# A fused sliding-window attention and long-convolution kernel: spectral sums in pairs, three third spectra by adding copies, quartered output tails, regrouped weights of v

## The chip, the core and the metric

The kernel runs on one core of a Trainium2 chip. A core has five engines that work side by side, each through its own queue in order: TensorE (PE in the profile, with its weight loads as PEld), VectorE (DVE), ScalarE (ACT), GpSimd (POOL) and SyncE (SP), which here only issues transfers. Matmul results land in PSUM; everything else lives in the on-chip memory or in HBM. The metric is the device time of one execution in microseconds.

## What is computed

Two independent parts, concatenated on the last axis. B = 1, S = 2048, D = 576.

```python
# A: 32 heads of 18; query s sees keys s, s-2, ..., s-14
qkv = x @ wqkv                                  # 2048 x 576 times 576 x 1728
logits = einsum("bhsd,bhswd->bhsw", q, kg) * scale     # w = 8 gathered keys
attn = softmax(where(mask, logits, -1e9))
a = einsum("bhsw,bhswd->bhsd", attn, vg) -> (s, 576) @ wo

# B: H3-like long convolution, per channel
k_shift = sum over t of k[s - t] * shift_k[:, t]       # 4 taps
kv = k_shift * v
y = irfft(rfft(kv, 4096) * rfft(ssm_k, 4096))[:2048] + kv * ssm_D
b = q * y
out = concatenate([a, b], axis=-1)
```

## The kernel before

**Part B in blocks.** Time is cut into four blocks of 512. DVE makes kv of a block (`taps`, L558 to L562), PE and ACT fold it (`mirror`, L570 and L571) and make its spectrum with cosine and sine tables (`x_spectrum`, L692; ACT writes it at L695, names fx0 to fx3). The four filter blocks are folded (`fold_filter`, L615 to L620) and transformed (`filter_spectrum`, L589 and L590, ACT at L635); a spectrum is turned from one block to the next by an accumulating copy on POOL's queue (`turn_filter`, L649). A spectrum has two parts of HB = 2304 elements per partition, and a third, their sum. Products of two spectra are then three elementwise products (parts one, two and three) in place of four, as in the three-multiplication form of a complex product. Where a block first needs its third part, DVE adds it (L1122): in three pieces of 768 for block 0, in one add of 2304 for the x spectra 1, 2, 3 and the filter spectra 1, 2, 3.

**The spectral stage.** Output block j needs the products of x block i with filter block j - i for all i up to j, in three thirds t of the channels: 30 products, in the order j, t, i. `products` (L985) is one DVE instruction of 3 x 768 elements into one of three buffers `pr`. `sums` (L1006) adds the three parts with 16 matmuls of 64x64 tiles, four at a time in the array's quarters, into two accumulators in PSUM; on the last i of a third, ACT copies both out (L1019; DVE the very last, L1017). `inverse` (L1038, last block's end L1057) and its back turn (L1079, L1065) make the time signal, and DVE multiplies it with q (L1092, at the end L1047). q is loaded by POOL's queue (L974, L976) and the result stored by SP's.

**Part A.** Projections of q, k and v (`project`, bodies at L360 and L364, 64-row tails at L371 and L377; `dest` gives the place). q and k use 128-column weight tiles. For v (comp 2) the weights are read in steps of nine, 64 columns at a time, straight from the loaded matrix (`wa`), so that channels of one residue mod 9 lie together and a v tile holds the rows in the order that the attention needs; two such 64-column tiles run side by side. Logits are DVE products of q and shifted k (L745) summed by PE (L754), softmax runs on DVE and ACT (L773 to L789), the attention weights are spread to all rows by SP's copies (L824), DVE multiplies with v (L846), PE sums (`weigh`, L862 and L876), and `output` multiplies with wo: L915 for 128 rows, `tails` at L907 for the 64 rows that are left, as two matmuls of 64 rows by 128 columns. ACT copies out (L922) into one of two buffers `st` behind wo in `qk`, and ACT's queue stores (L926).

**What sets the order.** Everything on one engine runs in the order in which the program issues it. DVE's list is the backbone. PE work that may be moved (projections, spectra, inverses, outputs) stands in a deque `units`; at each call of `until()` the next number of the table `PLACES` says how many of them are issued there. `FKS` and `FXS` mix filter spectra, x spectra and v's projections in that deque. `need(label)` issues units until none of that label is left. In the spectral stage the products run LEAD = 2 ahead of the sums, and `sums` calls `until()` once per product:

```python
for n, (j, t, i) in enumerate(todo):
    produce(n + LEAD)
    if (t, i) == (0, 0):
        need(f"inv{j - 2}")
    r = sums(j, t, i, *prs.pop(n))
```

Of the kernel before, what the change touches and what calls it, by code (L numbers as in the profile page):

```python
# [16 lines left out]
PSUM = bass.MemoryType.PSUM  # L17

PLACES = (
    16, 8, 5, 17, 0, 2, 0, 5, 2, 2, 1, 2, 8, 1, 0, 10, 0, 2, 3, 4, 2, 1, 2, 1, 2, 1, 0, 4, 3, 2, 12, 0, 4, 5, 2,  # L20
    2, 2, 2, 7, 1, 0, 2, 2, 0, 1, 0, 1, 0, 0, 1, 0, 2, 2, 1, 6, 1, 0, 2, 0, 2, 0, 1, 2, 0, 4, 1, 0, 1, 0,
)

FKS = (
    4, 0, 0, 3, 2, 0, 0, 0, 0, 0, 0, 0, 0, 0, 0, 0, 0, 0, 0, 0, 0, 0, 0, 0, 0, 0, 0, 0, 0, 0, 0, 0, 0, 0,
)
FXS = (
    6, 4, 3, 0, 0, 0, 0, 3, 2,
)


# [6 lines left out]
def kernel(  # L38
# [13 lines left out]
    nc = tc.nc  # L52
# [75 lines left out]
    def wa(kb, a):  # L128

        return view(xw, w_at(kb, 2) + a, [[9, 64]])  # L130

    def load_w(eng, comp, to=None):
        low, high = (to[:, 0:4, :], to[:, 4, :]) if to is not None else \
# [221 lines left out]
    def project(comp, jj):  # L355
        def body(ps, ct, jj, jp, first):
            for kb in range(4):
                se = dict(start=(kb == 0 and not first), stop=(kb == 3 and first))
                if ct < 4 and comp < 2:
                    nc.tensor.matmul(ps[:, jp, :], wq(kb, comp, 128 * ct, 128), xT(kb, 1024 * jj + 512 * jp, 512), **se)  # L360
                    continue
                for e in range(2):
                    w = wa(kb, min(2 * ct + e, 8)) if comp == 2 else wq(kb, comp, 512, 64)
                    nc.tensor.matmul(ps[64 * e:64 * e + 64, jp, :], w, xT(kb, 1024 * (jj if ct < 4 else e) + 512 * jp, 512),  # L364
                                     tile_position=(0, 64 * e), **se)

        def tails(ps, ct, jj, first):
            se = dict(start=first, stop=not first)
            if ct < 4 and comp < 2:
                for r in range(2):  # L370
                    nc.tensor.matmul(ps[:, r, :], wq(4, comp, 128 * ct, 128)[64 * r:64 * r + 64],  # L371
                                     x5(jj)[64 * r:64 * r + 64], tile_position=(64 * r, 0), **se)
                return
            for e in range(2):
                w = wa(4, min(2 * ct + e, 8)) if comp == 2 else wq(4, comp, 512, 64)
                for r in range(2):
                    nc.tensor.matmul(ps[64 * e:64 * e + 64, r, :], w[64 * r:64 * r + 64],  # L377
                                     x5(jj if ct < 4 else e)[64 * r:64 * r + 64], tile_position=(64 * r, 64 * e), **se)

        def unit(ct, jj, jp, first, box):  # L380
            t, o, pad = dest(comp, ct)
            if jp == 0:
                box["ps"] = bank2("ps_proj", "A")
                if first:
                    tails(box["ps"], ct, jj, True)
            ps = box["ps"]
            body(ps, ct, jj, jp, first)
            if jp == 0:
                clk["P"] += 1.15 if first else 0.9
                return  # L390
            if not first:
                tails(ps, ct, jj, False)
            pe(0.9 if first else 1.15, "A", 1.02)
            nc.scalar.activation(view(t, o + pad + 1024 * jj, [[512, 2], [1, 512]]), ps[:], ACT.Copy)  # L394
            if ct == 4 and comp > 0:
                nc.scalar.dma_start(view(t, o, [[1, PAD]])[64:128, :], view(t, o + 1024, [[1, PAD]])[0:64, :])

        for ct in range(4) if jj < 2 else [4]:
            first = ct % 2 == 1 if ct < 4 else comp == 1
# [251 lines left out]
    def turn_filter(m):  # L651
        for part in range(2):
            add_half(Ks, k_at(m, part), k_at(m - 1, part))

    for i in range(NBL):
        r = taps(i)
        until()
        if i < 2:
            load_k(i + 2)
            load_v(i + 2)  # L660
        if i == 1:
            load_filter(0)
            load_w(nc.sync, 2)
            for m in range(1, NBL):
                load_filter(m)
        if i == 1:
            nc.scalar.preload_act_table_set("natural_log_exp_and_others")
# [217 lines left out]
    spread(1)  # L885
    spread(2)

    wo = view(qk, 13312, [[2 * D, 2], [D, 2], [1, D]])
    woh = view(qk, 13312 + 4 * D, [[1, D]])
# [9 lines left out]
    def output(j, sb, h):  # L899

        hh, o = sb // 2, 128 * (sb % 2)
        ps = bank2("ps_wo", "A")

        def tails(first):
            for r in range(2):
                x = 64 * ((r + j) % 2)
                nc.tensor.matmul(ps[:, r, 0:HD], oTh(hh, r)[x:x + 64, o:o + 128],  # L907
                                 woh[x:x + 64, HD * h:HD * h + HD], start=first, stop=not first,
                                 tile_position=(x, 0))

# [69 lines left out]

    def products(j, t, i):

        pr = view(*((av, 0), (v, 6912), (qk, 9216))[npr[0] % 3], [[QTR, 3], [1, QTR]])
        npr[0] += 1
        r = dve(3 * QTR, lambda: nc.vector.tensor_tensor(  # L985
            pr, view(xw, HB * XG[i] + QTR * t, [[HB, 3], [1, QTR]]),
            view(Ks, k_at(j - i, 0) + QTR * t, [[HB, 3], [1, QTR]]), ALU.mult))
        return pr, r

    acc = {}  # L990

    def sums(j, t, i, pr, ready):

        until()
        m = j - i
        for r in range(2):
            sign = ((1, 1), (-1, 1), (-1, -1), (1, -1))[m][r]
# [111 lines left out]
    LEAD = 2  # L1109
    prs = {}  # L1110

    def produce(n):
        if n < len(todo):
            j, t, last = todo[n]
            for i in range(last + 1):
                need(f"fx{i}")
            due(1.0)
            for new, tile_, at in ((last == 0, Ks, k_at(j, 0)), (last == j, xw, HB * XG[j])):
                if new and (j == 0 or t == 0):
                    at, w = (at + QTR * t, QTR) if j == 0 else (at, HB)  # L1120
                    a, b, c = (view(tile_, at + HB * part, [[1, w]]) for part in range(3))
                    dve(w, lambda: nc.vector.tensor_tensor(c, a, b, ALU.add))  # L1122
# [5 lines left out]
    for n in range(LEAD):  # L1128
        produce(n)
    for n, (j, t, i) in enumerate(todo):  # L1130
        produce(n + LEAD)
        if (t, i) == (0, 0):
# [45 lines left out]
```

## Time and profile before

| | |
|---|---|
| median of 3 runs | 221.6 us (221.13 to 221.75) |
| the profiled execution | 221.13 us, its span 219.4 us |
| PE busy | 206.3 us, 94% of the span |
| DVE busy | 200.3 us, 91% |
| ACT busy | 151.6 us, 69% |
| POOL busy | 48.9 us, 22% |
| TensorE clock | 1.0 of full speed over the span |
| moved by DMA | 32.59 MB, mean 149 GB/s |

The span is what the profiler sees of the program on the core; 1.7 us lie around it. Busy times add up the durations of an engine's instructions. A matmul's duration holds its way through the array, so a busy PE may still have been waiting; how far one start is from the next is the better measure. "Idle before" a group is the engine's idle time ahead of its instructions, with what ended it.

The stages, read from the timelines: tables, taps, projections of q and k to about 57 us; logits and softmax of both halves with filter and x spectra and v's projections between them to about 124 us; weighing and outputs to about 157 us; the spectral stage to about 212 us; the last gate and stores.

### The profile page before, as it was taken

The page shows a single profiled execution, that of the slowest core. Times are in us where ns is not written, and L with a number is a line of the kernel's source. Part 1 is how long each engine was busy: PE and PEld are TensorE (multiplying, and loading weights), DVE is VectorE, ACT ScalarE, POOL GpSimd, SP SyncE. Part 2 cuts the span into 40 slices and gives each one's busy share as a digit, 9 for nine tenths or more (in the row PEclk, how much of TensorE's full clock was granted, in tenths as well). Part 3 has the DMA queues.
Part 4 walks back from the last instruction along what each step waited for, and adds up shares of the span by engine and source line. Part 5 has one row for each costly group of instructions (what it writes and reads, how often), then busy time and mean ns, then how long its engine had stood idle before and what let it go on. Part 6 is the DMA issues. An engine that isn't in the chain of part 4 may idle for free.

```text
span 219.4 us, 5341 instructions
## 1 busy us (share of the span) xinstructions
PE 206.3 (94%) x2262; PEld 119.1 (54%) x2266; DVE 200.3 (91%) x159; ACT 151.6 (69%) x218; POOL 48.9 (22%) x93
## 2 busy tenths in 40 slices
PE   7999899999699999999999999999979999999891
PEld 3543344444455556565576777555546666666560
DVE  7969999999989949899898699999999999999982
ACT  3699766896686799965359888755487776756530
POOL 8989800000320206220640000000240001130000
PEclk9999999999999999999999999999999999999999
DMA  6999987999150035999999485481282103580034
GB/s 211 269 282 276 266 286 253 158 200 253 28 87 4 0 54 82 189 178 221 226 249 236 59 232 133 68 183 55 74 249 74 40 4 108 172 251 13 3 100 115
DMA packets 32295, 32.59 MB, mean 149 GB/s; under 512 B 17136, under 2 KB 28016, under 8 KB 32272
## 3 DMA queue, kind: packets, MB, share of 16 engines
q1 hardware_dynamic: 25902, 21.93, 41.2%
q0 software_dynamic: 3744, 7.82, 17.8%
q10 hardware_dynamic: 2626, 2.52, 3.4%
q8 instruction: 17, 0.28, 0.5%
q14 instruction: 6, 0.05, 0.1%
HBM read 13.11 MB, written 4.72 MB: 81 GB/s over the span
## 4 chain that ended last, share of the span: by engine, by line
PE 72%; ACT 15%; DVE 7%; issue 3%; DVEq 0%; ACTq 0%
PE ps_proj L364 10%; PE ps_proj L360 7%; PE ps_acc L862 7%; PE ps_wo L915 6%; PE ps_z L1006 6%; PE ps_inv L1038 5%; PE ps_fx L692 4%; PE ps_log L754 4%; PE ps_fk L589 3%; PE ps_proj L482 3%; ACT Ks L635 2%; ACT xw L695 2%; PE ps_rev L615 2%; ACT qk L394 2%; PE ps_proj L377 2%
## 5 line engine op out<-in xcount | busy, mean ns | idle before, releaser
L745 DVE TENSOR_TENSOR av<-qk 128x4096 bf16<-128x4096 bf16 (+1 forms) x20 | 40.5, 2074 | 4.3 <-PE ps_log L754 4.2
L360 PE MATMUL ps_proj<-xw 128*128 128x512 bf16 x93 | 22.6, 380 | 0.8 <-ACT qk L394 0.5
L364 PE MATMUL ps_proj<-xw 128*64 128x512 bf16 x176 | 23.0, 396 | 0.0
L1019 ACT ACTIVATE av<-ps_z 128x768 bf16<-128x768 f32 x23 | 17.4, 809 | 5.3 <-PE ps_z L1006 5.3
L695 ACT ACTIVATE xw<-ps_fx 128x576 bf16<-128x576 f32 x32 | 18.5, 665 | 2.0 <-PE ps_fx L692 2.0
L974 POOL DMA_DIRECT2D TB<-in_B_q_dram x4 | 3.0, 742 | 75.7 <-DVE qk L846 45.4
L635 ACT ACTIVATE Ks<-ps_fk 128x576 bf16<-128x576 f32 x32 | 18.3, 660 | 1.7 <-PE ps_fk L590 1.5
L394 ACT ACTIVATE qk<-ps_proj 128x1024 bf16<-128x1024 f32 x14 | 14.4, 1027 | 7.0 <-PE ps_proj L371 3.7
L364 PEld LDWEIGHTS <-xw 128*64 128x64 bf16 x176 | 14.7, 180 | 7.3 <-issue 5.2
L915 PE MATMUL ps_wo<-qk 128*128 128x288 bf16 x128 | 18.1, 287 | 0.4 <-ACT qk L866 0.4
L692 PE MATMUL ps_fx<-xw,TB 64*128 64x288 bf16 x256 | 17.8, 283 | 0.2 <-ACT xw L571 0.2
L589 PE MATMUL ps_fk<-Ks,TB 128*128 128x384 bf16 x64 | 17.2, 327 | 0.1
L394 ACT ACTIVATE v<-ps_proj 128x1024 bf16<-128x1024 f32 x9 | 9.2, 1025 | 11.4 <-PE ps_proj L377 7.0
L561 DVE TENSOR_TENSOR xw<-xw,tB 128x2304 bf16<-128x2304 bf16 x12 | 16.3, 1358 | 0.4
L1038 PE MATMUL ps_inv<-av,TI 128*128 128x288 bf16 (+1 forms) x112 | 16.1, 292 | 0.6 <-ACT av L1019 0.6
L558 DVE TENSOR_TENSOR tB<-kj,skb 128x2304 bf16<-128x2304 bf16 x12 | 16.3, 1356 | 0.3
L620 POOL DMA_DIRECT2D Ks<-Ks x4 | 5.0, 1242 | 50.8 <-ACT Ks L618 50.8
L590 PE MATMUL ps_fk<-Ks,TB 128*128 128x192 bf16 x64 | 15.7, 246 | 0.0
L692 PEld LDWEIGHTS <-TB 64*128 64x128 bf16 x256 | 12.1, 94 | 6.5 <-issue 4.3
L922 ACT ACTIVATE qk<-ps_wo 128x576 bf16<-128x576 f32 x16 | 10.4, 650 | 7.3 <-PE ps_wo L907 4.5
L862 PE MATMUL ps_acc<-av,ident 64*64 64x512 bf16 x160 | 15.3, 378 | 0.1
L1041 ACT ACTIVATE v<-ps_inv 128x576 bf16<-128x576 f32 (+1 forms) x14 | 9.5, 675 | 8.3 <-PE ps_inv L1038 8.3
(187 smaller groups left out, 455.2 us busy)
## 6 DMA issues: line engine op xcount, KB each, us to landing
kj<-in_B_k_dram SPq DMA_DIRECT2D x7, 504.0 KB, 5.4
Ks<-Ks POOLq DMA_DIRECT2D x6, 576.0 KB, 8.3
TB<-av SPq DMA_DIRECT2D x12, 256.0 KB, 5.2
vt<-in_B_v_dram SPq DMA_DIRECT2D x8, 288.0 KB, 4.3
out_dram<-qk ACTq DMA_DIRECT2D x8, 288.0 KB, 2.4
Ks<-av SPq DMA_DIRECT2D x8, 256.0 KB, 5.1
xw<-in_A_wqkv_dram SPq DMA_DIRECT2D x3, 576.0 KB, 5.6
Ks<-in_A_x_dram SPq DMA_DIRECT2D x2, 576.0 KB, 5.2
```

Source lines behind the costliest of these rows:

```text
L360: nc.tensor.matmul(ps[:, jp, :], wq(kb, comp, 128 * ct, 128), xT(kb, 1024 * jj + 512 * jp, 512), **se)
L364: nc.tensor.matmul(ps[64 * e:64 * e + 64, jp, :], w, xT(kb, 1024 * (jj if ct < 4 else e) + 512 * jp, 512), tile_position=(0, 64 * e), **se)
L394: nc.scalar.activation(view(t, o + pad + 1024 * jj, [[512, 2], [1, 512]]), ps[:], ACT.Copy)
L589: nc.tensor.matmul(o[:, 0:2], w, rhs[:, 0:2], start=start, stop=stop)
L635: nc.scalar.activation(view(Ks, k_at(m, cs ^ (m & 1)) + 96 * gi, [[768, 3], [384, 2], [1, 96]]), acc3(ps), ACT.Copy, scale=(PSG, MSG)[cs][ ...
L692: nc.tensor.matmul(ps[:, pm, 0:HD], TX[64 * pm:64 * pm + 64, c, 128 * gi:128 * gi + 128], kv[64 * pm:64 * pm + 64, c, HD * h:HD * h + HD], ...
L695: nc.scalar.activation(view(xw, HB * XG[i] + 96 * gi + 1152 * h, [[HB, 2], [384, 3], [1, 96]]), view(ps, 0, [[512, 2], [96, 3], [1, 96]]), ...
L745: r = dve(1024 * nj, lambda: nc.vector.tensor_tensor(view(prod, 0, [[256 * nj, 4], [256, nj], [1, 256]]), view(t, o + 256 * hh, [[0, 4], [ ...
L862: nc.tensor.matmul(acc[64 * o:64 * o + 64, h, :], ident[64 * h:64 * h + 64, 64 * h:64 * h + 64], view(P, 256 * u, [[2048, 2], [1, 256]])[6 ...
L915: nc.tensor.matmul(ps[:, r, 0:HD], oT(hh, j + 2 * r, t)[:, o:o + 128], wo[:, t // 2, t % 2, HD * h:HD * h + HD], start=(t == 0 and h == 0) ...
L1019: nc.scalar.activation(y, z, ACT.Copy)
L1038: nc.tensor.matmul(ps[:, c, 0:n], TI[:, sl, pm, 128 * c:128 * c + 128], Yall[:, j % 2, pm, sl, c0:c0 + n], start=(pm == 0 and sl == 0), st ...
```

## The change

It has five parts.

- **Sums in groups of two.** Neighbouring products of one third are grouped (i even with the i behind it; the very last product stands alone). `until()` is called once per group, then the group's sums are issued one behind the other. Products are made up to two behind the end of the group.
- **A fourth `pr` buffer** at `qk` 9216 + HB.
- **Third spectra of x 2, x 3 and filter 3 by copies.** SP copies part one into the third's place, then POOL's queue issues an accumulating copy that adds part two. For x they are issued in the weighing stage, after all units of that spectrum; for the filter between the first two loads of q. DVE's adds for these three fall away.
- **Output tails in quarters**: four matmuls of 64 rows by 64 columns in place of two of 64 by 128. wo and the first `st` lie further back in `qk`; the second `st` is in `TB`.
- **v's weights regrouped.** They are loaded to a spare place in `Ks`, and five POOL copies bring them to their old place with the residues mod 9 together. v's projections then use the 128-column path of q and k (a body of one matmul, tails of 64x128); only the last 64 channels stay in 64-column tiles.

The tables `PLACES`, `FKS` and `FXS` have new numbers, so movable PE work is issued at other points. The core of the diff:

```diff
     def body(ps, ct, jj, jp, first):
-                if ct < 4 and comp < 2:
+                if ct < 4:
...
-                    w = wa(kb, min(2 * ct + e, 8)) if comp == 2 else wq(kb, comp, 512, 64)
+                    w = wq(kb, comp, 512, 64)
...
+    def third(t, at):
+
+        given.add((t is xw, at))
+        nc.sync.dma_start(half(t, at + 2 * HB), half(t, at))
+        add_half(t, at + 2 * HB, at + HB)
+
+    def third_x(i):
+        need(f"fx{i}")
+        third(xw, HB * XG[i])
+
+    def third_k(m):
+        third(Ks, k_at(m, 0))
+
+    raw = view(Ks, k_at(0, 0), [[D, 5], [1, D]])
...
-            load_w(nc.sync, 2)
+            load_w(nc.sync, 2, raw)
             for m in range(1, NBL):
                 load_filter(m)
+            for kb in range(5):
+                nc.gpsimd.tensor_copy(view(xw, w_at(kb, 2), [[64, 9], [1, 64]]), view(raw, D * kb, [[1, 9], [9, 64]]))
...
         def tails(first):
             for r in range(2):
                 x = 64 * ((r + j) % 2)
-                nc.tensor.matmul(ps[:, r, 0:HD], oTh(hh, r)[x:x + 64, o:o + 128],
-                                 woh[x:x + 64, HD * h:HD * h + HD], start=first, stop=not first,
-                                 tile_position=(x, 0))
+                for z in (0, 64):
+                    nc.tensor.matmul(ps[z:z + 64, r, 0:HD], oTh(hh, r)[x:x + 64, o + z:o + z + 64],
+                                     woh[x:x + 64, HD * h:HD * h + HD], start=first, stop=not first,
+                                     tile_position=(x, z))
...
-        st = view(qk, 13312 + 5 * D + 2 * D * (nst[0] // 2 % 2), [[D, 2], [1, D]])
+        st = view(*((qk, WO + 5 * D), (TB, 2 * HB))[nst[0] // 2 % 2], [[D, 2], [1, D]])
...
     steps(pvs, 1)
     spread(5)
+    third_x(2)
     steps(pvs, 4)
+    third_x(3)
...
-        pr = view(*((av, 0), (v, 6912), (qk, 9216))[npr[0] % 3], [[QTR, 3], [1, QTR]])
+        pr = view(*((av, 0), (v, 6912), (qk, 9216), (qk, 9216 + HB))[npr[0] % 4], [[QTR, 3], [1, QTR]])
...
-    def sums(j, t, i, pr, ready):
+    def sums(j, t, group):
 
         until()
+        for i, pr, ready in group:
+            out = sum_of(j, t, i, pr, ready)
+        return out
...
     load_q(0)
+    third_k(3)
     load_q(1)
...
-                if new and (j == 0 or t == 0):
+                if new and (j == 0 or t == 0) and (tile_ is xw, at) not in given:
...
+    for group in groups:
+        while made_to < min(group[-1] + 3, len(todo)):
+            produce(made_to)
+            made_to += 1
+        j, t, i = todo[group[-1]]
+        if (t, todo[group[0]][2]) == (0, 0):
             need(f"inv{j - 2}")
-        r = sums(j, t, i, *prs.pop(n))
+        r = sums(j, t, [(todo[n][2],) + prs.pop(n) for n in group])
```

More of the change, by code (lines that the diff above doesn't have):

```diff
@@ L19 @@
 PLACES = (
-    16, 8, 5, 17, 0, 2, 0, 5, 2, 2, 1, 2, 8, 1, 0, 10, 0, 2, 3, 4, 2, 1, 2, 1, 2, 1, 0, 4, 3, 2, 12, 0, 4, 5, 2,
-    2, 2, 2, 7, 1, 0, 2, 2, 0, 1, 0, 1, 0, 0, 1, 0, 2, 2, 1, 6, 1, 0, 2, 0, 2, 0, 1, 2, 0, 4, 1, 0, 1, 0,
+    16, 6, 9, 18, 0, 2, 1, 3, 4, 0, 4, 0, 4, 4, 1, 10, 0, 2, 2, 5, 1, 1, 2, 1, 1, 2, 0, 4, 3, 2, 11, 0, 5, 5, 0,
+    4, 2, 2, 9, 1, 1, 2, 2, 3, 2, 1, 0, 4, 1, 6, 5, 3, 0, 1, 6, 1, 1, 0,
 )
 FKS = (
-    4, 0, 0, 3, 2, 0, 0, 0, 0, 0, 0, 0, 0, 0, 0, 0, 0, 0, 0, 0, 0, 0, 0, 0, 0, 0, 0, 0, 0, 0, 0, 0, 0, 0,
+    6, 0, 0, 0, 3, 0, 0, 0, 0, 0, 0, 0, 0, 0, 0, 0, 0, 0, 0, 0, 0, 0, 0, 1, 0, 0, 0, 0, 0, 0, 0, 0, 0, 0,
 )
 FXS = (
-    6, 4, 3, 0, 0, 0, 0, 3, 2,
+    6, 3, 1, 0, 3, 2, 0, 0, 7,
 )
@@ L126, in wq @@
         return view(xw, w_at(kb, comp) + c0, [[1, n]])
-    def wa(kb, a):
-        return view(xw, w_at(kb, 2) + a, [[9, 64]])
     def load_w(eng, comp, to=None):
@@ L368, in tails @@
             se = dict(start=first, stop=not first)
-            if ct < 4 and comp < 2:
+            if ct < 4:
                 for r in range(2):
@@ L374, in tails @@
             for e in range(2):
-                w = wa(4, min(2 * ct + e, 8)) if comp == 2 else wq(4, comp, 512, 64)
+                w = wq(4, comp, 512, 64)
                 for r in range(2):
@@ L653, in turn_filter @@
             add_half(Ks, k_at(m, part), k_at(m - 1, part))
+    given = set()
+    def third(t, at):
[8 more added lines that the diff above has]
+    raw = view(Ks, k_at(0, 0), [[D, 5], [1, D]])
     for i in range(NBL):
@@ L886 @@
     spread(2)
-    wo = view(qk, 13312, [[2 * D, 2], [D, 2], [1, D]])
-    woh = view(qk, 13312 + 4 * D, [[1, D]])
+    WO = 18512 - 7 * D
+    wo = view(qk, WO, [[2 * D, 2], [D, 2], [1, D]])
+    woh = view(qk, WO + 4 * D, [[1, D]])
     for e in range(2):
@@ L990, with sum_of @@
     acc = {}
-    def sums(j, t, i, pr, ready):
+    def sums(j, t, group):
         until()
+        for i, pr, ready in group:
+            out = sum_of(j, t, i, pr, ready)
+        return out
+    def sum_of(j, t, i, pr, ready):
         m = j - i
@@ L1106 @@
     load_q(0)
+    third_k(3)
     load_q(1)
     clk["P"] = clk["D"]
-    LEAD = 2
-    prs = {}
+    groups = []
+    for n, (j, t, i) in enumerate(todo):
+        if i % 2 and (j, t, i) != todo[-1]:
+            groups[-1].append(n)
+        else:
+            groups.append([n])
+    prs, made_to = {}, 0
     def produce(n):
@@ L1126, in produce @@
                     late.popleft()[1]()
[L1128 to L1132, printed above, removed]
+    for group in groups:
[4 more added lines that the diff above has]
+        if (t, todo[group[0]][2]) == (0, 0):
             need(f"inv{j - 2}")
-        r = sums(j, t, i, *prs.pop(n))
+        r = sums(j, t, [(todo[n][2],) + prs.pop(n) for n in group])
         new = []
```

## The prediction, made before the changed kernel was run

> **What bounds the kernel now.** I read the page's busy line first, then the chain that ended last, then the table of stretches of 10 us, and last the timelines of VectorE (DVE), TensorE (PE) and GpSimd (POOL).
>
> ```profile
> PE 206.3 (94%) x2262; PEld 119.1 (54%) x2266; DVE 200.3 (91%) x159; ACT 151.6 (69%) x218; POOL 48.9 (22%) x93
> PE 72%; ACT 15%; DVE 7%; issue 3%; DVEq 0%; ACTq 0%
> ```
>
> Two engines are nearly full, and the chain runs over PE for 72% of the span. That alone would make DVE work free. The stretches say otherwise (columns: window, us, then busy us and instructions of PE, PEld, DVE, ACT, POOL, then clock, DMA share, GB/s):
>
> ```profile
> 120.00:130.00 10.00, 9.83 (x144) 7.04 (x140) 8.22 (x6) 8.35 (x15) 0.00 (x0) 1.00 0.65 140
> 140.00:150.00 10.00, 9.94 (x142) 5.87 (x136) 10.00 (x5) 5.58 (x9) 0.00 (x0) 1.00 0.67 139
> 180.00:190.00 10.00, 10.00 (x144) 6.74 (x142) 10.00 (x8) 7.06 (x11) 1.94 (x3) 1.00 0.41 119
> 200.00:210.00 10.00, 8.50 (x151) 5.32 (x142) 10.00 (x9) 5.16 (x8) 0.00 (x0) 1.00 0.01 2
> ```
>
> From 130 us to 210 us DVE has no free time at all, while PE falls to 8.5 of 10 at the end. DVE's timeline names its last wait (start, duration, instruction; in brackets the idle time before it):
>
> ```profile
> 122.63 1.23 DVE L789 TENSOR_TENSOR av<-av,xw 128x2048 bf16<-128x2048 bf16 x1 [1.74 <-ACT xw L787]
> 123.77 4.49 DVE L846 TENSOR_TENSOR av<-Ks,v 128x4096 bf16<-128x4096 bf16 x2
> ```
>
> After 122.63 no instruction of DVE shows an idle time until 211 us. So in the spectral stage (157 to 212 us) the first limit is DVE's list of work, and PE keeps up with some 5 us to spare. Before 124 us it is the reverse: DVE waits 8.4 us in all between 57 and 124 us (nine waits of 0.2 to 2.1 us on PE or ACT), so there DVE has slack and PE or ACT leads.
>
> **Part 1: third spectra by DMA.** Three adds of 2304 elements leave DVE (third x spectra 2 and 3, third filter spectrum 3). What one is worth is the step from its start to the next start, since the product behind it depends on it:
>
> ```profile
> 196.68 1.35 DVE L1122 TENSOR_TENSOR xw<-xw 128x2304 bf16<-128x2304 bf16 x1
> 198.13 1.36 DVE L985 TENSOR_TENSOR av<-xw,Ks 128x2304 bf16<-128x2304 bf16 x1
> ```
>
> 198.13 - 196.68 = 1.45 us; the other two are 1.46 (178.53 to 179.99, 191.41 to 192.87). Three make **4.4 us of DVE** in the stage that DVE limits. In their place stand three copies on SP's queue and three accumulating copies on POOL's. Rows: the 256 KB copies from SBUF to SBUF land in 5.2 us and the 576 KB accumulations in 8.3; for a 576 KB plain copy I take 5.2 to 8.3. SP's queue is free after the last spread is issued (143.0), and nothing else is due on it until 182.6. So x spectra 2 and 3 are whole by about 143 + 2 x 8.3 + some 3 of queueing = 163, and are needed at about 174 and 188. The filter's copy is behind these on SP; its accumulation stands on POOL behind q's first load (issued 157.6 to 159.6), so it lands by 170 and is needed at 188. q's second load, now behind it on POOL, lands by 175 and is needed at the gate at 188.9. Cost: nothing; that cover is 11 us or more each time. If it were gone, DVE would wait one for one.
>
> **Part 2: PE.** No column of matmul work goes. v's projections change from pairs of 128x64 tiles to whole 128x128: the pairs step 0.214 us, the whole ones (L360) 0.216, so nothing. Output tails go from two 64x128 to four 64x64: two of the old step 0.126 and four of the 64x64x288 kind (L1079) 0.123, nothing again. What changes is how often the array's tile shape changes. In the timeline:
>
> ```profile
> 170.29 0.33 PE L1006 MATMUL ps_z<-v,ident 64*64 64x384 bf16 x4
> 170.45 0.33 PE L1006 MATMUL ps_z<-v,identn 64*64 64x384 bf16 x4
> 170.72 1.15 PE L1038 MATMUL ps_inv<-av,TI 128*128 128x288 bf16 x8
> 171.80 0.36 PE L1006 MATMUL ps_z<-qk,identn 64*64 64x384 bf16 x4
> ```
>
> Four 64x64 matmuls step 0.16; the step to the first 128x128 is 0.27. Eight of these step 0.123, so the next shape could come at 171.70 and comes at 171.80. Each change of shape costs 0.1 us. Counting them in the two orders of instructions gives 152 before and 143 after: 0.85 us of PE, 0.5 of it (5) between the first and last spectral sum. The pairs of sums save most of these, since inverse transforms now stand between groups.
>
> PE's sum for that stretch (160.80 to 211.59, 50.8 us): 480 sum matmuls in fours of 0.163 = 19.5; 112 of inverses (96 x 0.123 + 16 x 0.163) = 14.4; outputs 56 x 0.123 + 0.9 = 7.7; back turns 1.5; 33 changes x 0.094 = 3.1; in all 46.1, so 4.7 us idle. After the change it is 45.7: without any idle time the last sum would end at 206.5, 5.1 earlier. DVE's last product ended at 209.69; less 4.4 it ends at 205.3, and its sum (0.65) at 206.0 at the earliest. So the two engines now meet, and **the gain of the tail is at most 5.1 us**.
>
> How much idle stays? The largest waits before were these kinds:
>
> ```profile
> 162.32 0.36 PE L1006 MATMUL ps_z<-v,ident 64*64 64x384 bf16 x4 [0.67 <-ACT av L1019]
> 204.62 0.36 PE L1006 MATMUL ps_z<-v,ident 64*64 64x384 bf16 x4 [0.40 <-DVE v L985]
> ```
>
> The first kind (1.3 us from 161.4 to 163) comes from two sums of block 0 back to back while ACT empties their banks one after the other; in the new order an output step stands between them. The second kind (2.2 us from 200.9 to 206) is PE out of products at the end; DVE would now be 4.4 ahead there, and a fourth buffer lets it be. Against that, a group may wait for its second product. I leave 1.2 us idle: **tail 3.9 us earlier**. Its ends are 5.1 (no idle) and 0.5 (all 4.7 us of idle stay, and only the shape changes are won).
>
> **Part 3: v's weights.** The load now goes to a spare place in Ks, lands as before at 49.5 (last issue at 44.1, 5.4 to land), and five POOL copies of 576 elements, read in steps of nine, regroup it. No such copy is in the trace. The rows nearest to it:
>
> ```profile
> 18.89 1.36 DVE L561 TENSOR_TENSOR xw<-xw,tB 128x2304 bf16<-128x2304 bf16 x1
> 21.67 1.36 DVE L561 TENSOR_TENSOR xw<-xw,tB 128x2304 bf16<-128x2304 bf16 x1
> 17.67 1.33 POOL L284 COPY flip<-flip 128x128 bf16<-128x128 bf16 x1
> 21.00 0.79 POOL L292 COPY identn<-identn 128x128 bf16<-128x128 bf16 x1
> ```
>
> Both copies end (19.00, 21.79) 0.11 us after a DVE instruction starts, whatever their length: most of it is waiting for DVE. So 128 elements run in some 0.11 us and 576 in 0.5 (lower end); a memset of 1728 took 1.53, 0.51 for 576; if all of the longest 128-element copy (1.44) were running, 6.5 (upper end). I take 0.5 each with one turn of DVE per copy, 1.39: the five end near 57, when the first fold accumulation was issued (57.76), and no later engine waits. DVE steps 1.39 beside POOL copies (17.49 to 18.89) and 1.40 without (27.08 to 28.48), so it loses nothing to 128 elements; for 576 it may lose up to 0.5 per copy, 2.5 in all, ahead of the fold matmuls at 58.42. DVE has 8.4 us of slack behind that, PE waits at 58.9 to 60.2 anyway. I put **0.5 us lost**, ends 0 and 2.5.
>
> [...]
>
> Other edits: wo's place and the second output buffer only move data, and their waits (wo on logits' products, at 105) end well before use (143): nothing. Logits' order on PE has its last group at 49.6 us of PE work after the first filter fold against 49.8: 0.2 us won, three shape changes fewer included.
>
> **Sum, against the profiled execution** (221.13 us, span 219.4, 1.7 around it): 3.9 + 0.2 - 0.5 = 3.6 less, span 215.8, **217.5 us**. That execution is the fastest of the three, 0.5 under the median of 221.6.
>
> **Rivals.**
> 1. *PE takes over* (0.18). For: PE's sum and DVE's list now differ by less than 1 us in the tail, and each wait on either engine now costs. Against: four buffers. If 3 us of idle stay (1.8 more), 219.3; if all 4.7, 220.9.
> 2. *POOL copies late, slower than before* (0.10). PE's queue reaches v's first projection, which needs all five parts, at about 69 us (68.0 before; in the new order two more x spectra stand ahead of it, two filter spectra behind). From 49.5 that leaves 3.9 us per copy; every us above costs PE, which is the leading engine there, five. At 4.6 the gain is gone; at 6.5 they end at 82 and the time is 217.5 + 13 = 230.5. For: the elements are read 18 bytes apart, and POOL rows of 1.3 to 1.4 us for 128 elements. Against: those rows end at DVE's boundaries.
> 3. *The third spectra don't come off DVE's path* (0.07): the copies land late and DVE waits as long as the adds took, 217.5 + 4.4 less what PE won, about 221.2. Against: 11 us of cover.
> 4. *POOL's copies hold DVE* (0.05): 0.5 us at each of five, 2.5 us ahead of the fold matmuls and the first logits, 219.5 if none of it meets slack. For: POOL's reads do wait for DVE's ends, so the two share something. Against: DVE's step of 1.39 beside them.
> 5. *No idle at all* (0.05): 216.0.
>
> **How the numbers follow.** The forecast has 0.55, 216.2 to 218.9. With rivals 1, 4 and 5 it reaches from 216.0 to 220.6, which holds 0.8. A measurement of this kernel tells about 0.3% (0.7 us) from no change. Faster by more: forecast, rivals 1, 4 and 5, 0.83; within: rival 3, 0.07; slower: rival 2, 0.10.
>
> **What would show it.** DVE's timeline: three adds of 2304 instead of six, no idle from about 123 on, last product ended near 205.5. PE: the last sum near 207.5, 143 changes of shape at 0.1. POOL: five copies between 49.5 and 58, and DVE's steps of 1.39 beside them no longer than 1.9. The accumulations of the third spectra landed by 175. I am wrong if DVE shows waits on PE in the tail of over 2 us, if v's projections start after 70, or if DVE waits for a queue of POOL.

## The result, and the profile after

The changed kernel takes **224.97 us** (median of 4 runs, 224.6 to 225.26) against 221.64: a ratio of 1.0154 [1.0132, 1.0176]. It is slower by 3.3 us, where 4.1 us less were forecast. The profiled execution took 225.26 us, its span is 223.5 us, and the mean granted TensorE clock 0.983.

From the page of the kernel after, the busy line, the TensorE clock in 40 slices and the chain by engine:

```profile
PE 206.5 (92%) x2218; PEld 112.2 (50%) x2218; DVE 201.7 (90%) x156; ACT 151.5 (68%) x218; POOL 63.8 (29%) x101
PEclk9999999999958999999999999999999999999999
PE 43%; DVE 20%; DMA 15%; ACT 10%; SPq 6%; issue 4%; DVEq 0%; ACTq 0%
```

DVE has three instructions less, as it should, and yet it is busy 1.4 us longer; POOL grew by 15 us. The clock row has a "5" and an "8" where before it had only nines. PE's share of the chain fell from 72% to 43%; DVE's rose from 7% to 20%, and DMA, which had none, has 15%.

Three dates split the span: the first logits' product on DVE (L760), the first spectral product (L1004) and the end of the last one. They are read from DVE's timelines:

| | first logits | first spectral | last ends | middle | tail |
|---|---|---|---|---|---|
| before | 57.32 | 157.99 | 209.69 | 100.67 | 51.70 |
| after | 62.87 | 163.14 | 213.79 | 100.27 | 50.65 |

So 5.55 us are lost ahead of the first logits, and only 1.45 of them come back. **Where they are lost**, DVE's and POOL's timelines tell (start, duration, instruction). Before, the first of five steps and the one behind them, and the first fold matmul on PE:

```profile
46.22 1.35 DVE L558 TENSOR_TENSOR xw<-kj,skb 128x2304 bf16<-128x2304 bf16 x1
53.04 1.36 DVE L558 TENSOR_TENSOR tB<-kj,skb 128x2304 bf16<-128x2304 bf16 x1
```

```profile
58.42 0.65 PE L570 MATMUL ps_fold<-xw,fold 128*128 128x288 bf16 x4
```

After, the same steps (three of the five are left out) and the copies:

```profile
45.59 1.36 DVE L558 TENSOR_TENSOR xw<-xw,vt 128x2304 bf16<-128x2304 bf16 x1
46.86 2.40 DVE L554 TENSOR_TENSOR xw<-kj,skb 128x2304 bf16<-128x2304 bf16 x1
51.62 2.30 DVE L557 TENSOR_TENSOR xw<-xw,tB 128x2304 bf16<-128x2304 bf16 x1
58.59 1.36 DVE L554 TENSOR_TENSOR tB<-kj,skb 128x2304 bf16<-128x2304 bf16 x1
```

```profile
46.12 11.22 POOL L680 COPY xw<-Ks 128x576 bf16<-128x576 bf16 x5 [19.76 <-DMA Ks<-in_A_wqkv_dram]
```

The five DVE steps that stand beside the five copies take 2.28 to 2.40 us, those on either side 1.36. By their starts the five take 11.73 us (46.86 to 58.59) against 6.82 before (46.22 to 53.04), 4.9 more. The rest of the 5.55 is a load of k for which DVE waited 0.68 us at 25 us in this execution, and not before. The fold matmuls wait for the last of these steps, and PE stands still. PE's timeline, and the stretches around it (window, us, then PE, PEld, DVE, ACT, POOL busy, then the clock):

```profile
57.79 0.41 PE L611 MATMUL ps_rev<-Ks,identn 128*128 128x288 bf16 x2
62.79 1.11 PE L566 MATMUL ps_fold<-xw,fold 128*128 128x288 bf16 x4 [4.59 <-DVE xw L558]
```

```profile
57.50:60.00 2.50, 0.70 (x6) 0.42 (x5) 2.43 (x3) 1.19 (x2) 1.96 (x2) 1.00 0.35 57
60.00:62.50 2.50, 0.00 (x0) 0.00 (x0) 2.46 (x2) 0.00 (x0) 1.43 (x4) 0.94 1.08 162
62.50:65.00 2.50, 1.95 (x8) 0.91 (x7) 2.37 (x2) 1.35 (x3) 0.00 (x0) 0.50 0.19 24
65.00:67.50 2.50, 2.30 (x18) 1.29 (x16) 2.36 (x2) 1.68 (x3) 0.00 (x0) 0.50 0.02 1
67.50:70.00 2.50, 2.50 (x28) 0.76 (x28) 1.27 (x1) 1.18 (x2) 0.00 (x0) 0.69 0.01 0
```

4.6 us without a matmul, and then the granted clock is half for some 6.8 us (62.2 to 69.0).

**The tail** answers the lines shown of before. The stretches of the kernel after:

```profile
180.00:190.00 10.00, 9.10 (x159) 5.95 (x159) 7.97 (x7) 7.76 (x13) 0.00 (x0) 1.00 0.02 6
200.00:210.00 10.00, 9.75 (x175) 6.82 (x173) 10.00 (x9) 6.53 (x11) 1.93 (x3) 1.00 0.46 134
```

DVE, full from 130 to 210 us before, now has 2 us free between 180 and 190; PE is at 9.75 of 10 near the end. DVE's timeline names its new waits, the table of ACT's waits (us in all, times, longest) and the table of transfers (KB each, us to land) name another:

```profile
182.87 1.36 DVE L1004 TENSOR_TENSOR v<-xw,Ks 128x2304 bf16<-128x2304 bf16 x1 [1.90 <-PE ps_z L1031]
194.60 1.36 DVE L1004 TENSOR_TENSOR av<-xw,Ks 128x2304 bf16<-128x2304 bf16 x1 [1.27 <-PE ps_z L1031]
```

```profile
ACT qk L939 <- DMA out_dram<-qk: 4.1, 2, 2.7
```

```profile
xw<-xw POOLq DMA_DIRECT2D x2, 576.0 KB, 7.6
out_dram<-qk ACTq DMA_DIRECT2D x4, 288.0 KB, 6.7
```

The other four of these stores, from `TB`, landed in 5.1 us. Before, ACT never waited for a store, and all eight were quick:

```profile
out_dram<-qk ACTq DMA_DIRECT2D x8, 288.0 KB, 2.4
```

### The profile page after: what moved, and what is told of

Read it like the earlier page. It is cut to its first block, busy times and chain, and to the rows that moved or that the text cites. A ratio compares the mean times of both kernels' runs of the same rounds, so it can differ in the third digit from the quotient of the medians.

```text
span 223.5 us, 5268 instructions
## 1 busy us (share of the span) xinstructions
PE 206.5 (92%) x2218; PEld 112.2 (50%) x2218; DVE 201.7 (90%) x156; ACT 151.5 (68%) x218; POOL 63.8 (29%) x101
## 4 chain that ended last, share of the span: by engine, by line
PE 43%; DVE 20%; DMA 15%; ACT 10%; SPq 6%; issue 4%; DVEq 0%; ACTq 0%
PE ps_z L1031 7%; DMA out_dram<-qk 7%; DVE xw L557 6%; DVE tB L554 6%; PE ps_inv L1063 6%; PE ps_proj L356 6%; PE ps_log L769 4%; PE ps_wo L932 4%; PE ps_fx L707 3%; ACT Ks L631 3%; DVE av L861 3%; DMA Ks<-in_A_x_dram 3%; PE ps_fk L585 3%; DMA kj<-in_B_k_dram 3%; SPq L229 3%
## 5 line engine op out<-in xcount | busy, mean ns | idle before, releaser
L760 DVE TENSOR_TENSOR av<-qk 128x4096 bf16<-128x4096 bf16 (+1 forms) x20 | 40.6, 2074 | 3.1 <-PE ps_log L769 2.8
L356 PE MATMUL ps_proj<-xw 128*128 128x512 bf16 x160 | 38.5, 380 | 0.5 <-ACT qk L390 0.5
L356 PEld LDWEIGHTS <-xw 128*128 128x128 bf16 x160 | 14.2, 98 | 19.9 <-issue 5.9
L707 PE MATMUL ps_fx<-xw,TB 64*128 64x288 bf16 x256 | 19.5, 295 | 0.6 <-ACT xw L710 0.3
L932 PE MATMUL ps_wo<-qk 128*128 128x288 bf16 x128 | 18.6, 287 | 0.4 <-ACT qk L881 0.4
L1004 DVE TENSOR_TENSOR qk<-xw,Ks 128x2304 bf16<-128x2304 bf16 x14 | 18.6, 1353 | 0.3
L557 DVE TENSOR_TENSOR xw<-xw,tB 128x2304 bf16<-128x2304 bf16 x12 | 18.2, 1514 | 0.4
L554 DVE TENSOR_TENSOR tB<-kj,skb 128x2304 bf16<-128x2304 bf16 x12 | 18.3, 1522 | 0.3
L680 POOL COPY xw<-Ks 128x576 bf16<-128x576 bf16 x5 | 11.2, 2290 | 19.8 <-DMA Ks<-in_A_wqkv_dram 19.8
L932 PEld LDWEIGHTS <-qk 128*128 128x128 bf16 x128 | 11.1, 98 | 7.5 <-issue 4.3
L1063 PEld LDWEIGHTS <-TI 128*128 128x128 bf16 x112 | 10.5, 98 | 8.1 <-issue 5.2
```

The source lines that it names most:

```text
L554: dve(2304, lambda: nc.vector.tensor_tensor(o, kj[:, 3 - j:7 - j, :], skb[:, 3 - j, :].unsqueeze(1).to_broadcast([128, 4, D]), ALU.mult))
L557: dve(2304, lambda: nc.vector.tensor_tensor(kv, kv, o, ALU.add))
L707: nc.tensor.matmul(ps[:, pm, 0:HD], TX[64 * pm:64 * pm + 64, c, 128 * gi:128 * gi + 128], kv[64 * pm:64 * pm + 64, c, HD * h:HD * h + HD], ...
L760: r = dve(1024 * nj, lambda: nc.vector.tensor_tensor(view(prod, 0, [[256 * nj, 4], [256, nj], [1, 256]]), view(t, o + 256 * hh, [[0, 4], [ ...
L1004: r = dve(3 * QTR, lambda: nc.vector.tensor_tensor(pr, view(xw, HB * XG[i] + QTR * t, [[HB, 3], [1, QTR]]), view(Ks, k_at(j - i, 0) + QTR ...
L1063: nc.tensor.matmul(ps[:, c, 0:n], TI[:, sl, pm, 128 * c:128 * c + 128], Yall[:, j % 2, pm, sl, c0:c0 + n], start=(pm == 0 and sl == 0), st ...
```

## The experiments

Four theories were to be told apart. **L**: each POOL copy holds the DVE step beside it, and the lateness is paid in full. **C**: the stall halves TensorE's clock, and that costs time of its own. **S**: the copies of the third spectra make the output stores late, which costs ACT. Against all of them: the pairs, buffers, quartered tails or new order lose the time. "After" below is the changed kernel. The ratios are to the kernel before as it was measured beside each run; its medians there went from 220.97 to 221.64 us, so a difference of some 0.7 us between the times of two runs is not told apart.

**1. Without the regrouping** (v's weights in their old order and with their old reads):

```diff
-                if ct < 4:
+                if ct < 4 and comp < 2:
...
-                    w = wq(kb, comp, 512, 64)
+                    w = wa(kb, min(2 * ct + e, 8)) if comp == 2 else wq(kb, comp, 512, 64)
...
-            load_w(nc.sync, 2, raw)
+            load_w(nc.sync, 2)
...
-            for kb in range(5):
-                nc.gpsimd.tensor_copy(...)
```

> The changed kernel without the regrouping of v's weights: they are loaded to their old place and read in steps of nine, and the five POOL copies are gone; all else as changed. Theory L (each POOL copy holds DVE for 0.95 us, five of them 4.7 us, and all of it reaches the end): DVE's steps in block 3's taps go back to 1.4 us, the first fold matmul of block 3 waits no more than 1 us for DVE, the clock stays at 1.0, and the spectral stage starts some 5 us earlier, near 157; time 219.5 to 220.5. Rival O (the new order of PE work and the groups cost the time, the POOL copies only fill slack): above 223.

Measured: 218.75 us, ratio 0.988 [0.9844, 0.9915]: faster than before, and 6.2 us under after. The tap steps are back to 1.36 us, the first logits' product starts at 57.28. The loss is the regrouping's, and more of it than L had put at 219.5 to 220.5: L had no price for the clock.

**2. Third spectra on DVE again, the regrouping kept** (`third` returns at once):

> The changed kernel with the three third spectra added by DVE again, and no copies for them; all else as changed, the POOL copies of the weights included. Theory S (the six copies of 576 KB share the DMA engines with the output stores, which then land in 6.7 instead of 2.4 us, so that ACT waits 4.1 us for its two output buffers and with it PE's sums and DVE): stores land in about 2.4 us, ACT's wait for them vanishes, DVE has 4.4 us more to do and 3 us less to wait; time within 1 us of the changed kernel, 224 to 226. If the copies cost nothing (rival: their cover held), the time rises by the whole 4.4, to 229.

Measured: 226.31, ratio 1.021 [1.0159, 1.0261], just above S's range and far below the rival's 229. The stores land in 3.0 and 2.2 us and ACT's wait for them is gone, but the kernel is no faster than after; the two intervals overlap. So the copies are not where the 3.3 us went. What the late stores cost by themselves this run doesn't say: it gives DVE three adds back, and in its trace the clock falls to 0.50 a second time, for 3.4 us from 205.8 on, after PE had waited 1.9 us for a product.

**3. Neither regrouping nor third copies**: pairs, four buffers, quartered tails and the new tables are left.

> The changed kernel with old weights of v and third spectra by DVE: what is left is pairs of sums, four buffers, quartered tails and the new tables. If L and S are the whole story, this is the kernel before within about 1 us, 220.5 to 222, with the spectral stage starting near 157. Rival O (order and groups cost by themselves): 223 or more.

Measured: 221.63, ratio 1.0018 [1.0001, 1.0034], the tail 51.97 against 51.70. These four edits alone gain nothing. In the profiled execution PE waits once for a product:

```profile
PE ps_z L1031 <- DVE v L1004: 1.9, 1, 1.9
```

That wait ends at 199.7, and from 199.9 on the granted clock is 0.50 for 3.4 us, here as in run 2. So the clock fell here after a wait of 1.9 us, less than half of the 4.6 in after.

**4. The stall kept, the clock held up.** 21 matmuls that nobody reads fill PE's wait ahead of block 3's folds:

```diff
+        if (i, n) == (3, 0):
+            ps = bank2("ps_idle", "B")
+            for _ in range(21):
+                nc.tensor.matmul(ps[:, 0, :], zeros[:, 0:128], zeros, start=True, stop=True)
```

> The changed kernel with 21 matmuls of 128x512 that nobody reads put ahead of the first fold matmul of block 3, where PE stood still for 4.6 us. Theory C (the granted clock fell to 0.5 from 62 to 68 us because PE stood still, and that costs some 3 us on top of DVE's lateness): the clock stays at 1.0 and the time falls to 222 to 223. Rival (DVE's lateness alone sets the time, PE would have waited anyway): 224.5 to 225.5.

Measured: 221.94, ratio 1.0036 [1.0014, 1.0058], at the lower edge of C's range and 3.0 us under after (2.6 by the ratios). The stretches of this kernel, where after had 0.00 and 1.95 of PE at a clock of 0.94 and 0.50:

```profile
60.00:62.50 2.50, 2.50 (x14) 1.25 (x13) 2.33 (x3) 0.00 (x0) 1.01 (x4) 1.00 1.05 157
62.50:65.00 2.50, 1.67 (x17) 0.99 (x17) 2.50 (x2) 2.34 (x4) 0.00 (x0) 1.00 0.04 4
```

The first logits still start at 62.25. So C holds: useless work that keeps the clock up is worth some 2 to 3 us, and the lateness itself is the rest. The two profiled executions bear out the lower end: from the first logits to the first spectral product this kernel takes 98.60 us and after 100.27, 1.7 more, and the tails are alike (50.75 and 50.65).

**5. Three staging buffers for the stores**, in the kernel before with the third spectra by copies:

```diff
-        st = view(qk, 13312 + 5 * D + 2 * D * (nst[0] // 2 % 2), [[D, 2], [1, D]])
+        st = view(*((qk, 13312 + 5 * D), (qk, 13312 + 7 * D), (TB, 2 * HB))[nst[0] // 2 % 3], [[D, 2], [1, D]])
```

> The kernel before, with the three third spectra formed by an SBUF copy and an accumulating copy, and with output stores that take turns over three staging buffers in place of two. Theory S (the accumulating copies make the output stores land late, so that ScalarE waits for its staging buffer; the same edit with two buffers showed 1.6 us of that wait, the kernel before 0): with a third buffer that wait falls below 0.3 us, and the time is 1.0 to 1.6 us below the same kernel with two buffers, about 217.3. Rival (TensorE or VectorE sets the pace of the tail, and ScalarE's wait lies beside it): ScalarE's wait is gone too, but the time is that of two buffers within 0.3 us.

Measured: 220.81, ratio 0.9993 [0.9976, 1.001]; with two buffers (run 8) 221.49, 1.002 [0.9979, 1.0061]. ACT's wait for stores went from 1.2 us to none, and the two times are not told apart, so no cost of the wait is seen. S's 217.3 took for granted a gain of the copies that run 8 doesn't show.

**6. The regrouping on ACT**, two copies behind block 2's taps and three behind block 3's:

```diff
-            for kb in range(5):
-                nc.gpsimd.tensor_copy(...)
...
+        if i > 1:
+            for kb in ((0, 1), (2, 3, 4))[i - 2]:
+                nc.scalar.activation(view(xw, w_at(kb, 2), [[64, 9], [1, 64]]), view(raw, D * kb, [[1, 9], [9, 64]]), ACT.Copy)
```

> The kernel after, with the five regrouping copies of v's weights on ScalarE (two behind block 2's taps, three behind block 3's) in place of GpSimd. Theory L (a GpSimd copy holds the VectorE step beside it for about 0.95 us, and the 4.6 us that the fold then starts late let TensorE's clock fall): with no GpSimd copy the tap steps are back to 1.4 us, the taps end at about 57, the clock stays near 1.0, and the time is that of the kernel without the regrouping plus at most what ScalarE pays late, 218.7 to 220.5. Rival (the regrouping costs in itself, by the weights' reads, whichever engine does it): the time stays above 222.5.

Measured: 224.43, ratio 1.0163 [1.0127, 1.0198], in the rival's range and not in L's. DVE's steps are all 1.36 us and the first logits' product starts at 57.10, so the hold is POOL's doing. But the wait moved, to the engine that now copies. ACT's timeline and PE's waits in this kernel:

```profile
56.72 3.56 ACT L684 ACTIVATE xw<-Ks 128x576 bf16<-128x576 bf16 x3 [0.62 <-ACT qk L390]
```

```profile
PE ps_rev L611 <- ACT Ks L614: 3.8, 1, 3.8
```

A copy takes ACT 1.2 us, not the 0.65 that I had taken from its evictions of the same size, and three of them stand ahead of the reversals' evictions; PE waits 3.8 us, and its clock is 0.50 from 59.7 to 66.5 us here too. This run doesn't price the regrouping; it shows the same stall and clock drop made by another engine.

**7. The POOL copies read in order and scatter** in place of gathering:

```diff
-nc.gpsimd.tensor_copy(view(xw, w_at(kb, 2), [[64, 9], [1, 64]]), view(raw, D * kb, [[1, 9], [9, 64]]))
+nc.gpsimd.tensor_copy(view(xw, w_at(kb, 2), [[1, 64], [64, 9]]), view(raw, D * kb, [[9, 64], [1, 9]]))
```

> The kernel after, with the five GpSimd copies walking the source in order and scattering the result, in place of gathering the source and writing in order; elements and result are the same. If the hold of VectorE comes of the reads in steps of 18 bytes, it falls from 0.95 us a copy to 0.5 or less, the fold comes 2.3 us earlier or more, and the time is 221 to 223. If it is a price by the element or by the instruction, whatever its order, the tap steps beside the copies stay at 2.3 to 2.4 us and the time at 224.5 to 225.5.

Measured: 228.62, ratio 1.0346 [1.0323, 1.0368]: neither of the two. POOL's and DVE's timelines:

```profile
45.86 15.77 POOL L680 COPY xw<-Ks 128x576 bf16<-128x576 bf16 x5 [18.29 <-DMA Ks<-in_A_wqkv_dram]
```

```profile
49.32 3.28 DVE L554 TENSOR_TENSOR tB<-kj,skb 128x2304 bf16<-128x2304 bf16 x1
62.24 1.36 DVE L554 TENSOR_TENSOR tB<-kj,skb 128x2304 bf16<-128x2304 bf16 x1
```

Scattered writes, 128 bytes apart, are dearer here than gathered reads, 18 apart: a copy adds 1.8 to 1.95 us to a step in place of 0.93 to 1.07, by starts 9.3 in five. So the price of these copies depends on how the copy walks, and DVE pays it. PE waits 8.6 us at the fold, and the clock is 0.50 for 10.2 us.

**8. Third spectra by copies alone**, in the kernel before (old tables, three buffers, single sums):

> The kernel before with one edit: the three third spectra of blocks 2 and 3 and of k's last formed by copies, no longer by VectorE. If that alone is the gain (the kernel without the regrouping was at 218.75 with it and at 221.6 without it), 218.5 to 219.0 and an interval wholly below 1. If the copies need the wider groups of the spectral stage to pay off (two products and four buffers, which absorb late stores), it comes out at 220 to 221.

Measured: 221.49, ratio 1.002 [0.9979, 1.0061]: no gain, and above both ranges. DVE's timeline there, with the longest of its waits:

```profile
192.45 1.36 DVE L1002 TENSOR_TENSOR av<-xw,Ks 128x2304 bf16<-128x2304 bf16 x1 [1.50 <-PE ps_z L1023]
```

Most of the 4.4 us that DVE saves in adds it spends waiting until PE has read a product's buffer: 3.5 us in five such waits. Before, there was none.

**9. POOL copies in order on both sides** (v's weights stay in their old order):

```diff
-nc.gpsimd.tensor_copy(view(xw, w_at(kb, 2), [[64, 9], [1, 64]]), view(raw, D * kb, [[1, 9], [9, 64]]))
+nc.gpsimd.tensor_copy(view(xw, w_at(kb, 2), [[1, D]]), view(raw, D * kb, [[1, D]]))
```

> The kernel after, with the five GpSimd copies of 576 elements reading and writing in order, so that v's weights stay in their old order and the value part of the output is another. Gathering, a copy adds 0.93 us to the VectorE step beside it (2.29 = 1.36 + 0.93), scattering it adds 1.79. If the copy's own time is the hold and its steps set that time, the copy in order adds 0.5 us or less, the fold waits 2.5 us in place of 4.6, the clock falls less or not at all, and the time is 219 to 222. If 0.9 us is the least that a copy of 576 takes, the time stays at 224 to 225.5.

Measured: 219.4, ratio 0.9934 [0.9907, 0.9961]. POOL's and DVE's timelines and PE's waits of this kernel:

```profile
45.61 7.92 POOL L680 COPY xw<-Ks 128x576 bf16<-128x576 bf16 x5 [18.18 <-DMA Ks<-in_A_wqkv_dram]
```

```profile
47.72 1.81 DVE L554 TENSOR_TENSOR tB<-kj,skb 128x2304 bf16<-128x2304 bf16 x1
49.56 1.70 DVE L557 TENSOR_TENSOR xw<-xw,tB 128x2304 bf16<-128x2304 bf16 x1
```

```profile
PE ps_fold L566 <- DVE xw L558: 1.2, 1, 1.2
```

The same 576 elements add 0.34 to 0.48 us to a step, 1.97 us in five by starts. PE waits 1.2 us, and in this execution the clock stays at 1.00. Five of the ten executions had a mean clock of 0.986 to 0.992 and took 219.66 to 221.2 us, the other five 218.73 to 219.13, so the median holds some lost clock; where it was lost no trace shows.

**10. Three product buffers**, in run 1's kernel (`npr[0] % 3`, and with one buffer less the products are made one ahead of a pair in place of two):

> The kernel after without the regrouping (218.75), with three product buffers in place of four, so that VectorE makes one product ahead of a pair and not two. Third spectra by copies alone gained nothing over the kernel before, and pairs with four buffers alone gained nothing; together they gained 2.9 us. If the fourth buffer is what lets VectorE use the time that it no longer spends on the third spectra, this is at 220.5 to 222. If the pairs are (fewer changes of TensorE's tile shape), it stays at 218.5 to 219.5.

Measured: 220.9, ratio 0.9993 [0.9971, 1.0015]. The gain of run 1 is gone; DVE's timeline has one wait of 3.6 us for a buffer:

```profile
177.33 1.36 DVE L1006 TENSOR_TENSOR qk<-xw,Ks 128x2304 bf16<-128x2304 bf16 x1 [3.63 <-PE ps_z L1033]
```

The fourth buffer, with the lead that it allows, is what lets DVE use its freed time.

**11. Sums one at a time**, in run 1's kernel:

> The kernel after without the regrouping (218.75), with the sums of one product at a time in place of two; four buffers stay. If the pairs are what turns the freed VectorE time into a gain, this is at 220.5 to 222. If the fourth buffer is, it stays at 218.5 to 219.5. Both this and three buffers slow: the two are needed together.

Measured: 233.43, ratio 1.0556 [1.053, 1.0582]. This doesn't test the pairs: the table that places PE's movable work has one number per group, so with more groups it runs ahead and ends early, and all the work behind it comes at other points. What the pairs are worth by themselves stays open.

**12. k's third spectrum on DVE**, x's two by copies, in run 1's kernel (no `third_k(3)`):

> The kernel after without the regrouping (218.75), with the third spectrum of k's last block on VectorE again, the two of x by copies. VectorE pays 1.46 us more, late in the tail, where it waits for TensorE 2.3 us; the copies beside the output stores are two in place of three. If VectorE's sum is the path: 219.5 to 220.5. If its idle time covers the sum and the stores land sooner: 218.0 to 219.0.

Measured: 218.72, ratio 0.9899 [0.9882, 0.9915], the same as run 1, and so is the tail, 49.07 against 49.05. DVE's waits for PE up to its last product fall from 1.56 us to 0.32, so the add is done in what was idle time. ACT's wait for a store in the tail falls from 1.57 us to 0.20 (it waits 1.97 for one at 153). The copy for k is worth nothing measurable here.

**13. The new projections without any copy** (v's weights plain, in their old order, straight to their place):

> The kernel after without the five copies: v's weights are loaded straight to their place and stay in their old order, so the value part of the output is another; v's projections use the new 128-column path. Its logits begin on time, at 57.3. From the first logits' product to the first spectral product the kernel with the old weights took 101.2 us, the one with copies in order, which began 1.8 late, 99.0. If the new path saves some 2 us there (whole tiles and fewer changes of shape on TensorE), this kernel takes 99 to 99.5 there too and is at 216.5 to 217.5. If the 2 us were only slack behind a late start, it takes 101 and is at 218.5 to 219.

Measured: 217.2, ratio 0.9809 [0.9793, 0.9825]; first logits at 57.32, middle 99.02, tail 49.84. On time, the new path is 2.15 us shorter in the middle than run 1 (101.17), so the projections are a gain and not slack. PE's timelines show it in the projections themselves. From the first matmul of a block of them to the next other matmul, eight of 128x64 take 1.06 us in run 1 (96.97 - 95.91), and the four whole ones in run 9, which has the same new path, take 0.95 (97.61 - 96.66). All ten blocks between the first logits and the first spectral product take 21.2 us in run 1 and 19.4 in run 9. It is a bound and no version, since it leaves out the regrouping of v's channels that the attention needs, as run 9 does. The fastest kernels that do the whole work are runs 1 and 12, and both are faster than the two kernels of this study.

Set beside each other, runs 13, 9, 7 and after differ in the copies alone, and run 4 is after with matmuls in the gap:

| copies | DVE held | clock | time | above run 13 |
|---|---|---|---|---|
| none (13) | 0 | full | 217.2 | 0 |
| in order (9) | 1.97 | full | 219.4 | 2.2 |
| gathered, PE kept busy (4) | 4.9 | full | 221.94 | 4.7 |
| gathered (after) | 4.9 | halved | 224.97 | 7.8 |
| scattered (7) | 9.3 | halved | 228.62 | 11.4 |

At a full clock the time follows the hold one for one, within what the times can tell apart; where the clock was halved, 2 to 3 us come on top.

## Why the prediction was wrong

**Part 3 failed, by the term "0.5 us lost, ends 0 and 2.5".** It measured 7.8 us, after against run 13: 4.9 of hold, and 2.9 that go with the halved clock. Of these 2.9 run 4 wins back all by the medians, and 1.7 in the middle by the two profiled executions, so the clock's price is 2 to 3 us and no better known. Three steps of its working broke.

- *The row.* "So 128 elements run in some 0.11 us and 576 in 0.5" scaled a copy of 128 elements that walks in order. For such copies it about holds: run 9 has 0.34 to 0.48. The copies of the change read 18 bytes apart and cost 0.93 to 1.07. The text named the steps of nine and then priced them at nothing; the upper end went only into rival 2, as lateness on POOL, and not into the hold. For the last steps it is 0.93 against 0.34, 2.7 times, for the same 576 elements.
- *Who is held.* The text saw that POOL waits for DVE and took most of the hold away from DVE, since it "loses nothing to 128 elements". In every run with such copies each DVE step beside one is longer by the copy's price: 2.29 is 1.36 + 0.93 and 3.15 is 1.36 + 1.79. (A copy's own time is not seen apart from this: POOL's rows hold its waits for DVE.) Rival 4 had the mechanism right, at 2.5 us and a chance of 0.05. That run 9, with copies in order, came out within 0.1 us of its 219.5 is partly luck, since its hold is 1.97 and not 2.5 and other terms were off too.
- *What stands behind.* "DVE has 8.4 us of slack behind that, PE waits at 58.9 to 60.2 anyway": the slack absorbed nothing of the hold (runs 13 and 9 take the same 99.02 us in the middle, and run 9 begins it 1.7 us later), since the fold and the first logits wait for these very steps. And the case of PE standing still long enough to lose its clock wasn't in the sum at all. PE's waits of before are under 1 us there, and no row showed a drop.

Rival 2, the one that ended slower, had the right instructions and the wrong victim: the copies ended at 57.3, long before v's projection, and PE waited for DVE at the fold. V's projections start at 75.1 us in place of 68.0, which the prediction named as a sign of being wrong, but in run 9, with the copies and without the stall, they start at 69.7.

**Part 1 was right in DVE's term, and wrong that the copies cost nothing.** Three adds left DVE, and the data were in time. But beside the 576 KB copies the output stores of the changed kernel land in 5.1 and 6.7 us in place of 2.4, a cover that I had not looked at. In runs 5 and 12 ACT's wait for them went without a gain. In after, where ACT waits 4.1 us in place of run 1's 1.6, what that costs was not tested by itself.

**The tail was mis-sized:** forecast 3.9 us earlier, measured 1.05 in the changed kernel (51.70 to 50.65), 1.9 in run 13 (49.84) and 2.65 in run 1 (49.05). DVE waits 3.2 us for PE's buffers there in the changed kernel, over the 2 us that the prediction named as a sign of being wrong, and near to rival 1. Why the tail differs among these three kernels stays open; ACT waits 4.1, 3.2 and 1.6 us for stores in them. Runs 3, 8 and 10 show what the forecast only assumed: less DVE work alone brings nothing (ratio 1.002), pairs and buffers alone nothing (1.0018), both together 2.9 us (run 3 to run 1). That fits two engines near their limit, each waiting for the other: DVE for a buffer in runs 8 and 10, PE for a product in run 3.

**The logits' stage was mis-sized the other way:** 0.2 us forecast, 1.65 measured (100.67 to 99.02 in run 13). I had found that v's projections step the same from one matmul to the next. Block by block they don't: 1.06 us for eight narrow ones against 0.95 for four whole ones, and 21.2 against 19.4 us in all, most of the 2.15 us between runs 1 and 13. Whether it is the changes of tile shape or the tails was not isolated.

These two errors nearly cancel, and that is luck: the forecast without its 0.5 for POOL is 217.0, and the change without the copies (run 13) takes 217.2.

## What to carry to other kernels

Price a copy on GpSimd by how it walks, on both sides (here 0.34 to 1.95 us for 576 elements), and charge its price to the VectorE step beside it (here TENSOR_TENSOR steps of 1.36 us without a copy); then look at which matmuls wait for that step. If they leave TensorE without work for some 2 us or more (the shortest wait here with a fall behind it was 1.9), look at the granted clock, add what its fall costs (here 2 to 3 us after a wait of 4.6), and try unread matmuls in the gap. Work taken from one of two engines that were both nearly full paid here only when the buffers between them allowed it to run ahead (218.75 us with four, 220.9 with three).

## What the hardware showed that I had not expected

- A GpSimd copy of 576 bf16 elements held VectorE 0.34 to 0.48 us in order (run 9), 0.93 to 1.07 with reads 18 bytes apart (after), 1.8 to 1.95 with writes 128 bytes apart (run 7). ScalarE took 1.2 us for the gathered one, 0.65 for an eviction of the same size (run 6).
- Waits of 0.8 and 1.2 us (before and run 9) left TensorE's clock at 1.00, and so did one of 1.3 in after's tail. Waits of 1.9 us in runs 2 and 3 were followed by 0.50 for 3.4 us, waits of 3.8, 4.3 and 4.6 us (runs 6, 2 and after) by 0.50 for 6.8, and one of 8.6 (run 7) by 0.50 for 10.2.
- With the 576 KB copies of the third spectra issued ahead of them, ACT's 288 KB stores to HBM landed in 3.6 to 7.0 us (medians of the runs), without them in 2.2 to 3.3. No run here shows why.
